# Attention and a gated MLP on one core: the early stage's operations held back and issued in one written order

## The chip, the cores and the metric

The kernel runs on one core of one Trainium2 chip. The time is the device time of one execution in microseconds (us). A core has five engines that run their own queues of instructions side by side and wait for one another by semaphores: TensorE (PE; its weight loads are listed apart as PEld), VectorE (DVE), ScalarE (ACT), GpSimd (POOL) and SyncE (SP), which issues most of the DMAs. A few DMAs are issued from ACT's queue.

## What is computed

Block-causal attention over 8 batches and 8 heads, 576 positions, head size 64, blocks of 64; its output, as 4608 tokens of width 512, goes through a gated MLP and an output projection.

```python
def _attn_ref(q, k, v):                      # (8, 8, 576, 64)
    scores = scale * np.matmul(q, k.transpose(0, 1, 3, 2))
    mask = block_i >= block_j                # blocks of 64 positions
    scores = np.where(mask, scores, -1000000000.0)
    scores = scores - np.max(scores, axis=-1, keepdims=True)
    attn = np.exp(scores)
    attn = attn / (np.sum(attn, axis=-1, keepdims=True) + 1e-09)
    return np.matmul(attn, v).astype(np.float32)

def _moe_ref(x, w1, w2, w3, w_out):          # x: (4608, 512)
    a = x @ w1
    b = x @ w2
    h = a * b @ w3
    return (h @ w_out).astype(np.float32)
```

The kernel folds the last two products: it computes `w3 @ w_out` once (1024 x 512), and the MLP then is `((x@w1)*(x@w2)) @ (w3@w_out)`.

## The kernel before

**Tiles and stages.** The work goes by pairs of heads, n = 0 to 31 (8 batches of 4 pairs); a pair has two halves, j = 0 and 1, one for each head. Pairs 0 to 3, the first batch, are the *early stage*: while they run, the weights arrive and are taken apart. From pair 4 on, the *late stage*, every step of attention is mixed with steps of the MLP of the batch before.

**Attention of a pair.** `shift_mask` casts k and q to bf16 (`kb`, `qd`, L166 on ACT), makes the block maxima of the scores in six groups of matmuls (`mx`, L192, in a ring of two `psq` banks), which DVE reduces into `m` (L196, L198). One transpose on PE (`mt`, L200) and a scaling on ACT (`ms`, L202) turn them into a row, and `shift` sends 2.2 KB of it by DMA into row slots of `qk0` and `qk1` (L218), so that the scores come out with the maximum taken off. These steps for pair n+1 stand within pair n. `prep_qk` makes the high and low parts of q and k (`qk0`, `qk1`: L166, DMAs L232 and L233, subtraction L235). The scores (`s`, L265, two banks `pss`) are two matmuls for each tile; the second reads the row that the DMA brought. ACT exponentiates them (in the early stage into `pe`, L273). In the early stage `pv_early` multiplies them with v in plain float32 (`x`, L304, one bank pair `psx`); `take_early` (L344 to L346) takes the sums and the result out, `norm` (L355 to L358) and `finish_x` (L367, L368) normalize and split it.

**Weights.** They come in 40 units of 512 KB (L143, issued on SP, ring `wraw` of 5), and each is put together by five steps of `load_w`: the scaled upper half (`wy`, ACT L150), a byte on ACT (L151) and one on POOL (L152) into one of two `wbits` tiles, and the join on DVE (L153). `w1` and `w2` are then split into two parts (POOL L161, DVE L162); `w_out` lies in `wo`, and `w3` in blocks `w`, two in the ring.

**The folded product.** `gen_prod` runs eight blocks m = 0 to 7 of eight matmuls each (L407, tiles `w0` to `w7`, two banks `psm`); `wh` and `wl` (L410 on ACT, L411 on DVE) take a block out.

**What sets the order.** PE's order is that of the program in the whole kernel (`manual_schedule` for PE alone): `EARLY_PLAN` says for each pair and half in which order the steps come, one letter a step; C is a step of the weights and W a quarter of a product block. The other four engines are ordered by the tile scheduler; the early stage's steps other than C and W run under `high_priority(offset=0)`. Buffers come from tile pools, which hand the next tile a buffer when its last user is done.

```python
            for step in EARLY_PLAN[n][j].split() if early else PLAN[j].split():
                if step in "CW":
                    fill(weights if step == "C" else prod, 1)
                    continue
                with tc.high_priority(offset=0) if early else nullcontext():
```

Of the kernel before, what the change touches and what calls it, by code (L numbers as in the profile page):

```python
# [8 lines left out]
F32 = mybir.dt.float32  # L9
# [7 lines left out]
AX = mybir.AxisListType  # L17
PSUM = bass.MemoryType.PSUM

P = 128  # L20
# [39 lines left out]
)  # L60

DELAY = 3

CAST = (0, 1, 1, 1)


@with_exitstack
def block_causal_attention__then__gated_mlp_kernel(ctx, tc, qkv, consts, ident_in, w1, w2, w3t, wout, out_t):
    nc = tc.nc
    w1, w2, w3t, wout = (w.bitcast(I32) for w in (w1, w2, w3t, wout))  # L70
# [30 lines left out]
    def load(n):  # L101
        t = raws.tile([P, RAW], F32, tag="raw", name=f"raw{n}")
        src = qkv[n // NPAIR, n % NPAIR]
        for cs in (slice(S, 2 * S), slice(0, S), slice(2 * S, RAW)) if n == 0 else (slice(0, RAW),):
            nc.sync.dma_start(out=t[:, cs], in_=src[:, cs])
        raw_of[n] = t

    load(0)
    for t, tag in enumerate(("tr", "x32")):
        cst = work.tile([P, S], F32, tag=tag, name=f"cst{t}")  # L110
# [27 lines left out]
    def load_w(dst, src):  # L138
        t = tl["early"].tile([P, 1024], I32, tag="wraw", name="wraw", bufs=5)
        y = tl["early"].tile([P, 512], F32, tag="wy", name="wy", bufs=4)  # L140
        bits = tl["bits"][tl["unit"] % 2]
# [32 lines left out]
    def shift_mask(n):  # L174
        r = raw_of[n]
        rqk = r[:, 0 : 2 * S].rearrange("p (t s) -> p t s", t=2)
        kb = work.tile([P, S], BF16, tag="kb", name=f"kb{n}")
# [4 lines left out]
        m = work.tile([P, 32], F32, tag="m", name=f"m{n}")  # L182

        groups = [((7, 0, 512),), ((8, 0, 512),), ((0, 0, 64), (6, 0, 448)), ((1, 0, 128), (5, 0, 384)),
                  ((2, 0, 192), (4, 0, 320)), ((8, 512, 576), (3, 0, 256))]
        for g, parts in enumerate(groups):
            t = ps_q.tile([P, 512], F32, tag="psq", name=f"mx{n}_{g}")
            at = 0
            done = []
            for i, a, b in parts:  # L190
                sc = t[:, at : at + b - a]
                nc.tensor.matmul(sc, qd[:, i, :], kb[:, a:b], start=True, stop=True)  # L192
                done.append((sc, 9 if a else i))
                at += b - a
            for sc, col in done:
                nc.vector.reduce_max(m[:, col : col + 1], sc, axis=AX.X)  # L196
            yield
        nc.vector.tensor_tensor(out=m[:, 8:9], in0=m[:, 8:9], in1=m[:, 9:10], op=ALU.max)  # L198
        mt = ps_q.tile([P, 512], F32, tag="psq", name=f"mt{n}")
        nc.tensor.transpose(out=mt[0:NB, 0:P], in_=m[:, 0:NB], identity=ident)  # L200
        ms = work.tile([64, P], F32R, tag="ms", name=f"ms{n}")[32 : 32 + NB]
        nc.scalar.mul(out=ms, in_=mt[0:NB, 0:P], mul=-1.0)  # L202
# [52 lines left out]
    def s_tile(n, j, parts, p_early):  # L255
        t = ps_s.tile([P, 512], F32, tag="pss", name=f"s{n}_{j}")
        at = 0
# [83 lines left out]
    def take_early(n, j, xps, x32, rr):  # L341
        o, x = own[j], oth[j]
        tr = work.tile([P, S], F32, tag="tr", name=f"tr{n}_{j}")
        nc.vector.transpose(tr[o], xps[x, 384:960])  # L344
        nc.vector.tensor_scalar_add(rr[o], tr[o].rearrange("p (b c) -> p b c", c=32)[:, :, 0], 1e-9)
        nc.scalar.copy(x32[o], xps[o, 384:960])  # L346
# [7 lines left out]
    def norm(n, x32, rr):  # L354
        nc.vector.reciprocal(rr, rr)  # L355
        rb = work.tile([P, S], F32, tag="tr", name=f"rb{n}")
        nc.vector.transpose(rb, rr.unsqueeze(2).broadcast_to([P, S // 32, 32]))
        (nc.gpsimd if n < 2 else nc.vector).tensor_tensor(out=x32, in0=x32, in1=rb, op=ALU.mult)  # L358

    def finish_x(n, x32):  # L360
        for h in range(2):
            at = (2 * n + h) % 12
            pool, bufs = (xpool, 8) if at < 8 else (tl["late"], 4)
            xh = pool.tile([P, HALF], F32R, tag="xh", name=f"xh{n}_{h}", bufs=bufs)
            xl = pool.tile([P, HALF], F32R, tag="xl", name=f"xl{n}_{h}", bufs=bufs)
            src = x32[:, h * HALF : (h + 1) * HALF]
# [7 lines left out]
    def gen_w(wp):  # L374
# [4 lines left out]
        def w3(m):  # L379
            assert done[0] >= m - 1  # L380
            t3_of[m] = wp.tile([P, NF, P], F32, tag="w3", name="w3", bufs=2)
            for h in range(2):
# [19 lines left out]
    def gen_prod():  # L402
        wo = tl["wo"]
        for m in range(NF):
            acc = ps_m.tile([P, 512], F32, tag="psm", name=f"w{m}")
            for k in range(NF):
# [61 lines left out]
    def pair(n):  # L468

        early = n < EARLY  # L470
        x32 = work.tile([P, S], F32, tag="x32", name=f"x32_{n}")
        rr = work.tile([P, S // 32], F32, tag="rr", name=f"rr{n}")
        part = None if early else work.tile([P, 2, S // 32], F32, tag="part", name=f"part{n}")
# [4 lines left out]
        for j in range(2):  # L478
            xps = ps_x.tile([P, 1024], F32, tag="psx", name=f"x{n}_{j}")
            p_early = wp.tile([P, 1600], F32, tag="pe", name=f"pe{n}_{j}") if early else None  # L480
            tiles = s_tiles(n, j, p_early)
            pvs = (pv_early if early else pv)(n, j, xps, p_early)
            delay = DELAY if n == NPAIR and j == 0 else 0
            for step in (EARLY_PLAN[n] if early else PLAN)[j].split():
                if step in "CW":
                    fill(weights if step == "C" else prod, 1)
                    continue
                with tc.high_priority(offset=0) if early else nullcontext():
                    if step == "S":
                        fill(tiles, 1)  # L490
                    elif step == "F":
                        if delay:
                            delay -= 1
                        else:
                            fill(mlp, 1)
                    elif step == "M":
                        fill(masks, 1)
                    elif step == "A":
                        fill(next_qk, 1)
                    elif step == "B":  # L500
                        fill(own_qk, 1)
                    elif step in "UV":
                        fill(pvs, 1)
                    elif step == "R":
                        sums(n, j, part)
                    elif step == "N" and early:
                        take_early(n, j, xps, x32, rr)
                    elif step == "N":
                        take(n, j, xps, x32)
                    elif step == "T":  # L510
                        if not early:
                            total(n, part, rr)
                        norm(n, x32, rr)
                        finish_x(n, x32)
                    elif step == "Q" and not last:
                        if n + 1 != NPAIR:
                            prep_v(n + 1, j)
                        if j == 1 and n + 2 < NN:
                            load(n + 2)
# [69 lines left out]
```

## Time and profile before

| | |
|---|---|
| time, median of 3 runs | 969.47 us (968.91 to 970.46) |
| the profiled execution's own time | 970.15 us |
| its span in the profile | 968.3 us |
| instructions | 18335 |
| DMA packets, bytes | 31303, 79.81 MB |

The profile is of one execution. Times in it are in us from the span's start. A row of the timeline gives start, duration, engine, line and operation, the output tile and its inputs (buffer numbers left out), partitions x elements, type and how many instructions the row stands for; in square brackets is how long the engine was idle ahead of it and what ended that. A float32 matmul on PE is listed as two records. "Granted clock" (PEclk) is the share of TensorE's full clock in that stretch.

### The profile page before, as it was taken

What the parts mean: (1) busy time and instruction counts of PE and PEld (TensorE: products, weight loads), DVE (VectorE), ACT (ScalarE), POOL (GpSimd) and SP (SyncE); (2) the same over time, 40 slices, a digit from 0 to 9 for tenths busy, and PEclk for the clock granted to TensorE, in tenths of its full rate; (3) what the DMA queues carried; (4) which work ended last, traced back from release to release, by engine and by line L of the source; (5) the groups of instructions that cost most, each with busy time, mean ns of one, the idle gap of its engine ahead of it and who ended that gap; (6) DMA issues with size and microseconds to landing.
All of it is one profiled execution on the core that took longest, in us unless ns stands there. A gap on an engine that the chain in (4) does not pass through costs nothing.

```text
span 968.3 us, 18335 instructions
## 1 busy us (share of the span) xinstructions
PE 938.8 (97%) x6624; PEld 878.7 (91%) x6624; DVE 692.3 (72%) x1230; ACT 556.6 (57%) x1451; POOL 617.5 (64%) x605
## 2 busy tenths in 40 slices
PE   3898899999999999999999999999999999999998
PEld 1454469999999999999999999999999999999998
DVE  6787767788777777787787777777887777774100
ACT  7768736556565556565656555565555656553221
POOL 6766737677766767677776767676777667672211
PEclk9899999999999999999999999999999999999999
DMA  8976512212212221321222222222122122100000
GB/s 303 305 230 204 158 51 64 86 32 72 76 58 82 65 88 52 88 65 47 66 76 64 71 81 64 78 61 88 33 69 75 58 82 64 50 13 26 7 20 26
DMA packets 31303, 79.81 MB, mean 82 GB/s; under 512 B 5356, under 2 KB 13676, under 8 KB 31212
## 3 DMA queue, kind: packets, MB, share of 16 engines
q1 hardware_dynamic: 29788, 76.26, 25.7%
q10 hardware_dynamic: 1424, 2.38, 1.0%
q8 instruction: 52, 0.85, 0.4%
q14 instruction: 39, 0.32, 0.1%
HBM read 50.76 MB, written 9.44 MB: 62 GB/s over the span
## 4 chain that ended last, share of the span: by engine, by line
PE 89%; ACT 3%; DVE 3%; POOL 2%; issue 1%; DMA 1%; ACTq 0%; SPq 0%; DVEq 0%; POOLq 0%
PE ab L426 42%; PE o L442 21%; PE s L265 9%; PE x L320 9%; PE mx L192 4%; PE w L407 2%; POOL wbits L152 1%; ACT wbits L151 1%; ACT wy L150 1%; PE x L304 1%; DVE m L196 1%; ACT pe L273 1%; DMA qk<-ms 1%; DVE w L153 0%; PE tot L337 0%
## 5 line engine op out<-in xcount | busy, mean ns | idle before, releaser
L286 POOL TENSOR_TENSOR rsum<-rsum,p 128x448 f32<-128x448 f32 x224 | 185.8, 829 | 86.8 <-ACT p L280 78.3
L283 DVE TENSOR_TENSOR pl<-p,ph 128x448 fp32r<-128x448 f32 x168 | 149.4, 903 | 59.9 <-ACT ph L281 59.0
L435 POOL TENSOR_TENSOR gl<-g,gh 128x288 fp32r<-128x288 f32 x128 | 114.4, 894 | 121.9 <-ACT gh L434 121.9
L265 PE MATMUL s<-qk 128*128 128x288 f32 (+4 forms) x768 | 155.2, 311 | 6.1 <-ACT pe L273 3.6
L235 POOL TENSOR_TENSOR qk<-raw,qk 64x1152 fp32r<-64x1152 f32 x58 | 155.0, 2673 | 8.6 <-issue 5.6
L426 PE MATMUL ab<-xh,w2h 128*128 128x288 f32 x512 | 153.8, 300 | 0.0
L442 PE MATMUL o<-gh,wh 128*128 128x288 f32 x512 | 153.6, 300 | 0.0
L426 PE MATMUL ab<-xh,w1h 128*128 128x288 f32 x512 | 151.1, 295 | 0.0
L426 PE MATMUL ab<-xl,w2h 128*128 128x288 f32 x512 | 151.0, 295 | 0.0
L426 PE MATMUL ab<-xl,w1h 128*128 128x288 f32 x512 | 151.0, 295 | 0.0
L426 PE MATMUL ab<-xh,w1l 128*128 128x288 f32 x512 | 150.9, 295 | 0.0
L426 PE MATMUL ab<-xh,w2l 128*128 128x288 f32 x512 | 150.9, 295 | 0.0
L442 PE MATMUL o<-gh,wl 128*128 128x288 f32 x512 | 150.9, 295 | 0.0
L442 PE MATMUL o<-gl,wh 128*128 128x288 f32 x512 | 150.8, 295 | 0.0
L434 ACT CAST gh<-g 128x288 fp32r<-128x288 f32 x128 | 55.4, 433 | 143.1 <-DVE g L433 143.0
L265 PEld LDWEIGHTS s<-qk 128*128 128x128 f32 (+1 forms) x768 | 116.0, 182 | 17.9 <-ACT pe L273 9.4
L281 ACT ACTIVATE ph<-s 128x288 fp32r<-128x288 f32 x336 | 131.5, 393 | 0.0
L196 DVE TENSOR_REDUCE m<-mx 128x1 f32<-128x64 f32 (+3 forms) x320 | 128.4, 447 | 2.2 <-PE mx L192 0.2
L280 ACT ACTIVATE p<-s 128x448 f32<-128x448 f32 x224 | 85.4, 381 | 51.2 <-PE s L265 50.4
L283 DVE TENSOR_TENSOR pl<-rsum,ph 128x288 fp32r<-128x288 f32 x112 | 75.6, 676 | 49.6 <-ACT ph L281 45.6
L320 PE MATMUL x<-ph,vs 128*128 128x128 f32 x336 | 110.4, 329 | 0.0
L433 DVE TENSOR_TENSOR g<-ab,a 128x288 f32<-128x288 f32 x128 | 56.6, 442 | 69.8 <-PE ab L426 69.0
(76 smaller groups left out, 2180.4 us busy)
## 6 DMA issues: line engine op xcount, KB each, us to landing
raw<-in_qkv SPq DMA_DIRECT2D x31, 896.0 KB
qk<-qk SPq DMA_DIRECT2D x108, 144.0 KB
out_t<-o SPq DMA_DIRECT2D x64, 144.0 KB
wraw<-in_w3t SPq DMA_DIRECT2D x16, 512.0 KB
wraw<-in_w SPq DMA_DIRECT2D x16, 512.0 KB
wraw<-in_wout SPq DMA_DIRECT2D x8, 512.0 KB
qk<-qk ACTq DMA_DIRECT2D x16, 144.0 KB
qk<-ms SPq DMA_DIRECT2D x54, 2.2 KB
```

What stands on the lines that cost most here:

```text
L196: nc.vector.reduce_max(m[:, col : col + 1], sc, axis=AX.X)
L235: (nc.gpsimd if "late" in tl or n * j else nc.vector).tensor_tensor(out=qk[j][o, 2:4], in0=rqk[o], in1=qk[j][o, 0:2], op=ALU.subtract)
L265: nc.tensor.matmul(t[ks, at : at + q1 - q0], qk[j][:, k, kr], qk[j][:, q, q0:q1], start=(s == 0), stop=(s == 1))
L280: nc.scalar.activation(p32, t[ks, at : at + w], AF.Exp, scale=SCALE)
L281: nc.scalar.activation(ph[ks, o : o + w], t[ks, at : at + w], AF.Exp, scale=SCALE)
L283: nc.vector.tensor_tensor(out=low, in0=p32, in1=ph[ks, o : o + w], op=ALU.subtract)
L286: nc.gpsimd.tensor_tensor(out=r, in0=r, in1=p32, op=ALU.add)
L320: nc.tensor.matmul(xps[:, to : to + w], v[:, c, :], pr[:, a : a + w], start=(u < 2 and s == 0), stop=(u in (0, len(PV) - 1) and s == len(p ...
L426: nc.tensor.matmul(t[:, 0:HALF], l[:, c, fs], r, start=(c == 0 and s == 0), stop=(c == NC - 1 and s == 2))
L433: nc.vector.tensor_tensor(out=g32, in0=acc[1][:, 0:HALF], in1=a32, op=ALU.mult)
L435: nc.gpsimd.tensor_tensor(out=gl[:, f, :], in0=g32, in1=gh[:, f, :], op=ALU.subtract)
L442: nc.tensor.matmul(t[:, 0:HALF], l[:, f, es], r[:, f, :], start=(f == 0 and s == 0), stop=(f == NF - 1 and s == 2))
```

## The change

In the early stage the name `nc` no longer stands for the core but for a recorder, `Held`. Each call on it is appended to a list and not issued; 761 calls are collected. Tiles are not made at that point either: `new` returns a `Later`, which is resolved when a held call that uses it is issued, and `slot` then gives it a buffer of a ring in turn: two for `raw`, `pss`, `psm`, `psq` and `w3`, five for `wraw`, four for `wy`, eight for `xh` and `xl`, one for all others. After the early stage's program has run through, all calls are issued in the order that `ORDER` lists, under `manual_schedule` for the other four engines, so that the order of each engine in this part is that of `ORDER`. The late stage follows with the real `nc`, as before. `high_priority` is gone. In the changed kernel every held call carries the line of `Held.__call__`, L123, and tiles of a ring have one name for all their uses (`psm` for `w0` to `w7`, `psq` for `mx` and `mt`, `psx` for `x`, `m` and `ms` without a number).

```diff
-from contextlib import ExitStack, nullcontext
+from contextlib import ExitStack
...
+OTHERS = {mybir.EngineType.Activation, mybir.EngineType.DVE, mybir.EngineType.Pool, mybir.EngineType.SP}
...
+ORDER = [int(k) for k in """
+0 10 1 2 11 3 6 12 9 44 58 46 48 13 71 63 53 41 40 72 68 14 93 43 5 15 42 20 21 16 70 7 47 76 79 22 45 23 4 59 17 18 49 19 32 33 8 50 34 28 29 35 30
...
+""".split()]
+
+RING = {"raw": 2, "pss": 2, "psm": 2, "psq": 2, "wraw": 5, "wy": 4, "w3": 2, "xh": 8, "xl": 8}
...
+class Later:
+
+    def __init__(self, make):
+        self.make, self.made = make, None
+
+    def get(self):
+        if self.made is None:
+            self.made = self.make()
+        return self.made
+
+    def __getitem__(self, key):
+        return Later(lambda: self.get()[key])
...
+class Held:
+
+    def __init__(self, target, calls):
+        self.target, self.calls = target, calls
+
+    def __getattr__(self, name):
+        return Held(getattr(self.target, name), self.calls)
+
+    def __call__(self, *a, **k):
+        self.calls.append(lambda: self.target(*map(got, a), **{n: got(v) for n, v in k.items()}))
...
-    nc = tc.nc
+    calls = []
+    nc = Held(tc.nc, calls)
+
+    rings = collections.defaultdict(list)
+
+    def new(pool, shape, dtype, tag, **k):
+        if not isinstance(nc, Held):
+            return pool.tile(shape, dtype, tag=tag, **k)
+        return Later(lambda: slot(pool, shape, dtype, tag, **k))
+
+    def slot(pool, shape, dtype, tag, name, **k):
+        ring = rings[tag]
+        n = RING.get(tag, 1)
+        t = ring[-n] if len(ring) >= n else pool.tile(shape, dtype, tag=tag, name=tag, **k)
+        ring.append(t)
+        return t
...
-                with tc.high_priority(offset=0) if early else nullcontext():
-                    if step == "S":
-                        fill(tiles, 1)
+                if step == "S":
+                    fill(tiles, 1)
...
     fill(weights, 100)
     fill(prod, 100)
+    with tc.manual_schedule(engines=OTHERS):
+        for k in ORDER:
+            calls[k]()
+    nc = tc.nc
+    raw_of.update((n, got(t)) for n, t in raw_of.items())
+    ms_of.update((n, got(t)) for n, t in ms_of.items())
+    x_of.update((k, tuple(map(got, t))) for k, t in x_of.items())
     wstack.close()
     open_late()
```

The order of the instructions at the places that matter most, first TensorE's at the end of pair 0, before (`s0_1`, `pe0_1`, `ve1` and `x0_1` are scores, exponentials, v and result of its half 1; `mt1` is the transpose of pair 1's maxima, `w0` the first block of the folded product):

```order
L265 MATMUL s0_1_322<-qk1_87 128x320 x2
L265 MATMUL s0_1_343<-qk1_87 128x192 x2
L265 MATMUL s0_1_343<-qk1_87 64x64 x2
L304 MATMUL x0_1_282<-pe0_1_283,ve1_157 128x128
L304 MATMUL x0_1_282<-pe0_1_283,ve1_157 128x448 x2
L200 MATMUL mt1_355<-ident_81,m1_211 9x128
L304 MATMUL x0_1_282<-pe0_1_283,ve1_157 128x320
L304 MATMUL x0_1_282<-pe0_1_283,ve1_157 128x192
L304 MATMUL x0_1_282<-pe0_1_283,ve1_157 128x64
L407 MATMUL w0_383<-wo_108,w3_298 128x512 x4
```

And now, where `w0` stands in the ring tile `psm_280` and `ve0` belongs to half 0 of pair 0:

```order
L123 MATMUL psx_210<-pe_202,ve0_97 128x320
L123 LDWEIGHTS qd_90
L123 MATMUL psq_138<-kb_119,qd_90 128x64
L123 LDWEIGHTS qd_90
L123 MATMUL psq_138<-kb_119,qd_90 128x256
L123 MATMUL psm_280<-wo_94,w3_274 128x512 x8
L123 MATMUL psq_141<-ident_81,m_150 9x128
L123 LDWEIGHTS qd_90
L123 MATMUL psq_138<-kb_119,qd_90 128x128
L123 MATMUL psm_312<-wo_94,w3_289 128x512
```

The whole first block stands now within PV of half 0, ahead of `mt1` and of all scores of half 1; the second block (`psm_312`) begins right behind it, one matmul at a time.

TensorE's order where the early stage ends and pair 4 begins (`mt4` is the transpose of pair 4's maxima, `s4_0` its first scores), before:

```order
L200 MATMUL mt4_1063<-ident_81,m4_914 9x128
L304 MATMUL x3_1_978<-pe3_1_979,ve1_157 128x320
L304 MATMUL x3_1_978<-pe3_1_979,ve1_157 128x192
L304 MATMUL x3_1_978<-pe3_1_979,ve1_157 128x64
L407 MATMUL w6_1031<-wo_108,w3_857 128x512 x4
L407 MATMUL w7_1095<-wo_108,w3_1034 128x512 x8
L265 MATMUL s4_0_1129<-qk0_86 128x288 x2
```

And now:

```order
L123 MATMUL psx_210<-pe_202,ve1_98 128x320
L123 MATMUL psx_210<-pe_202,ve1_98 128x192
L123 MATMUL psx_210<-pe_202,ve1_98 128x64
L123 MATMUL psm_312<-wo_94,w3_289 128x512 x8
L123 MATMUL psq_138<-ident_81,m_150 9x128
L340 MATMUL s4_0_929<-qk0_86 128x288 x2
```

The transpose has moved from ahead of PV's last three matmuls to behind the last block of the product, and stands directly ahead of pair 4's scores.

ScalarE's order at the same place (`ms4` is the scaled row, `vs0` and `vs1` are pair 4's v, `wh` the high part of a block of the folded product), before:

```order
L202 ACTIVATE ms4_1065<-mt4_1063 9x128
L218 DMA qk0_86<-ms4_1065 1x9x64
L346 COPY x32_3_872<-x3_1_978 64x576
L218 DMA qk1_87<-ms4_1065 1x9x64
L367 CAST xh3_0_1081<-x32_3_872 128x288
L410 CAST wh_84<-w6_1031 128x512
L367 CAST xh3_1_1085<-x32_3_872 128x288
L410 CAST wh_84<-w7_1095 128x512
L166 CAST vs0_1113<-raw4_831 128x5x64
```

And now:

```order
L123 COPY x32_109<-psx_210 64x576
L308 DMA qk1_87<-qk1_87 64x576
L123 CAST xh_891<-x32_109 128x288
L123 CAST xh_894<-x32_109 128x288
L123 CAST wh_84<-psm_312 128x512
L123 ACTIVATE ms_186<-psq_138 9x128
L241 CAST vs0_913<-raw_101 128x5x64
L123 DMA qk0_86<-ms_186 1x9x64
L241 CAST vs1_914<-raw_101 128x5x64
L293 DMA qk1_87<-ms_186 1x9x64
```

The scaling and its two DMAs stood ahead of `wh` of blocks 6 and 7; they stand now behind the last `wh`, and the casts of pair 4's v lie between them.

More of the change, by code (lines that the diff above doesn't have):

```diff
@@ L101, in load @@
     def load(n):
-        t = raws.tile([P, RAW], F32, tag="raw", name=f"raw{n}")
+        t = new(raws, [P, RAW], F32, tag="raw", name=f"raw{n}")
         src = qkv[n // NPAIR, n % NPAIR]
@@ L109, in block_causal_attention__then__gated_mlp_kernel @@
     for t, tag in enumerate(("tr", "x32")):
-        cst = work.tile([P, S], F32, tag=tag, name=f"cst{t}")
+        cst = new(work, [P, S], F32, tag=tag, name=f"cst{t}")
         nc.sync.dma_start(out=cst[0:D], in_=consts[:, t * S : (t + 1) * S])
@@ L138, in load_w @@
     def load_w(dst, src):
-        t = tl["early"].tile([P, 1024], I32, tag="wraw", name="wraw", bufs=5)
-        y = tl["early"].tile([P, 512], F32, tag="wy", name="wy", bufs=4)
+        t = new(tl["early"], [P, 1024], I32, tag="wraw", name="wraw", bufs=5)
+        y = new(tl["early"], [P, 512], F32, tag="wy", name="wy", bufs=4)
         bits = tl["bits"][tl["unit"] % 2]
@@ L176, in shift_mask @@
         rqk = r[:, 0 : 2 * S].rearrange("p (t s) -> p t s", t=2)
-        kb = work.tile([P, S], BF16, tag="kb", name=f"kb{n}")
+        kb = new(work, [P, S], BF16, tag="kb", name=f"kb{n}")
         cast(n, kb, rqk[:, 1, :], CAST[1])
@@ L181, in shift_mask @@
         yield
-        m = work.tile([P, 32], F32, tag="m", name=f"m{n}")
+        m = new(work, [P, 32], F32, tag="m", name=f"m{n}")
         groups = [((7, 0, 512),), ((8, 0, 512),), ((0, 0, 64), (6, 0, 448)), ((1, 0, 128), (5, 0, 384)),
@@ L186, in shift_mask @@
         for g, parts in enumerate(groups):
-            t = ps_q.tile([P, 512], F32, tag="psq", name=f"mx{n}_{g}")
+            t = new(ps_q, [P, 512], F32, tag="psq", name=f"mx{n}_{g}")
             at = 0
@@ L255, in s_tile @@
     def s_tile(n, j, parts, p_early):
-        t = ps_s.tile([P, 512], F32, tag="pss", name=f"s{n}_{j}")
+        t = new(ps_s, [P, 512], F32, tag="pss", name=f"s{n}_{j}")
         at = 0
@@ L342, in take_early @@
         o, x = own[j], oth[j]
-        tr = work.tile([P, S], F32, tag="tr", name=f"tr{n}_{j}")
+        tr = new(work, [P, S], F32, tag="tr", name=f"tr{n}_{j}")
         nc.vector.transpose(tr[o], xps[x, 384:960])
@@ L355, in norm @@
         nc.vector.reciprocal(rr, rr)
-        rb = work.tile([P, S], F32, tag="tr", name=f"rb{n}")
+        rb = new(work, [P, S], F32, tag="tr", name=f"rb{n}")
         nc.vector.transpose(rb, rr.unsqueeze(2).broadcast_to([P, S // 32, 32]))
@@ L404, in gen_prod @@
         for m in range(NF):
-            acc = ps_m.tile([P, 512], F32, tag="psm", name=f"w{m}")
+            acc = new(ps_m, [P, 512], F32, tag="psm", name=f"w{m}")
             for k in range(NF):
@@ L487, in pair @@
                     continue
-                with tc.high_priority(offset=0) if early else nullcontext():
-                    if step == "S":
-                        fill(tiles, 1)
[L491 to L519, printed above, removed]
@@ new lines, in pair @@
+                if step == "S":
+                    fill(tiles, 1)
+                elif step == "F":
+                    if delay:
+                        delay -= 1
+                    else:
+                        fill(mlp, 1)
+                elif step == "M":
+                    fill(masks, 1)
+                elif step == "A":
+                    fill(next_qk, 1)
+                elif step == "B":
+                    fill(own_qk, 1)
+                elif step in "UV":
+                    fill(pvs, 1)
+                elif step == "R":
+                    sums(n, j, part)
+                elif step == "N" and early:
+                    take_early(n, j, xps, x32, rr)
+                elif step == "N":
+                    take(n, j, xps, x32)
+                elif step == "T":
+                    if not early:
+                        total(n, part, rr)
+                    norm(n, x32, rr)
+                    finish_x(n, x32)
+                elif step == "Q" and not last:
+                    if n + 1 != NPAIR:
+                        prep_v(n + 1, j)
+                    if j == 1 and n + 2 < NN:
+                        load(n + 2)
```

22 lines of the change are left out of this document (13 added, 9 removed), and 19 rows, old and new, of the table ORDER.

## The prediction

> **What bounds the kernel now.** I read the page's busy shares and its chain first, then where TensorE (PE) waits.
>
> ```profile
> span 968.3 us, 18335 instructions
> PE 938.8 (97%) x6624; PEld 878.7 (91%) x6624; DVE 692.3 (72%) x1230; ACT 556.6 (57%) x1451; POOL 617.5 (64%) x605
> PE   3898899999999999999999999999999999999998
> PEclk9899999999999999999999999999999999999999
> PE 89%; ACT 3%; DVE 3%; POOL 2%; issue 1%; DMA 1%; ACTq 0%; SPq 0%; DVEq 0%; POOLq 0%
> ```
>
> PE is busy 97% of the span and makes up 89% of the chain that ended last. Each digit of the second row is one slice of 24.2 us, and the only slices below 9 are 0, 1, 3, 4 and the last one. In the view of PE's waits no wait of PE stands between 150 us and the end. So the time can change only before the late stage begins, or at its seam, and the late stage's own order is the same in both kernels. **The question is when its first scores (pair 4) start, and whether they run on.** In the profile of before that start is 136.24 us, the last row here (start, duration, engine, line, tile):
>
> ```profile
> 5.93 1.01 PE L192 MATMUL mx<-kb,qd 128*128 128x512 bf16 x2 [5.93 <-ACT qd L166]
> 20.80 0.61 PE L192 MATMUL mx<-kb,qd 128*128 128x512 bf16 x1 [4.24 <-ACT qd L166]
> 37.07 3.70 PE L407 MATMUL w<-wo,w 128*128 128x512 f32 x8
> 126.24 10.57 PE L407 MATMUL w<-wo,w 128*128 128x512 f32 x24
> 136.24 0.96 PE L265 MATMUL s<-qk 128*128 128x288 f32 x3
> ```
>
> What comes before is poor in work until the weights are there, and rich after. In the stretches below the columns are length, busy time and count of PE, weight load, DVE, ACT, POOL, then granted clock, DMA share, GB/s:
>
> ```profile
> 0.00:20.00 20.00, 4.91 (x15) 2.05 (x15) 13.07 (x21) 13.36 (x22) 13.36 (x20) 1.00 0.84 308
> 31.00:37.00 6.00, 5.23 (x17) 3.15 (x17) 4.90 (x7) 3.46 (x9) 4.37 (x4) 0.72 1.02 326
> 46.00:51.00 5.00, 5.00 (x17) 3.21 (x17) 2.57 (x5) 4.36 (x8) 1.86 (x2) 0.69 0.65 200
> 66.76:136.24 69.48, 63.90 (x215) 33.30 (x215) 52.24 (x81) 42.97 (x87) 40.40 (x38) 1.00 0.52 154
> ```
>
> In the first 20 us PE works 4.91 us, and the DMA is 0.84 full with the weights. From 66.76 us on PE is the limit; what it has before is wasted. Its waits between the first product at 37.07 and the late stage are these (total, times, longest), 8.5 us together:
>
> ```profile
> PE mx L192 <- DVE m L196: 3.0, 3, 2.0
> PE mx L192 <- ACT qd L166: 2.1, 1, 2.1
> PE s L265 <- ACT pe L273: 1.9, 3, 1.2
> PE s L265 <- DMA qk<-ms: 1.5, 2, 1.0
> ```
>
> **The change, part by part.** The set of early instructions is the same; what changes is their place, on all five engines. I therefore count when the first product can start, what PE has left from there, and what the end costs.
>
> *First product.* w0 needs both halves of w3's first block. They were written on VectorE (DVE) by 28.48 (27.81+0.67) and 30.93 (30.26+0.67):
>
> ```profile
> 27.81 0.67 DVE L153 SCALAR_TENSOR_TENSOR w<-wy,wbits 128x512 int32<-128x512 int32 x1
> 28.51 0.79 DVE L344 STREAM_TRANSPOSE tr<-x 64x576 f32<-64x576 f32 x1
> 29.60 0.40 DVE L345 TENSOR_SCALAR rr<-tr 64x18 f32<-64x18 f32 x1
> 30.26 0.67 DVE L153 SCALAR_TENSOR_TENSOR w<-wy,wbits 128x512 int32<-128x512 int32 x1
> 31.32 1.60 DVE L235 TENSOR_TENSOR qk<-raw,qk 64x1152 fp32r<-64x1152 f32 x1
> ```
>
> Before, w0 waits in PE's order behind the scores and the attention-times-values product (PV) of half 1. In the new order it stands behind mask 1 and ahead of its transpose mt1. On DVE the 1.60 of pair 1's subtraction now stands ahead of the second w3 half, and the transpose and sum of pair 0 (0.79, 0.40) behind it: 30.93+1.60−1.19 = 31.3. The first half has one 0.67 weight step less ahead. PE runs the eight matmuls in order of k, so the first four can start on the first half. I take 30.7 for the start, between 28.5 (first half as before, no more ahead of it) and 33.7 (31.3 with another 1.60 and 0.79 of DVE ahead of it). This fills PE time in the stretch 31 to 37, where the clock was 0.72.
>
> *What is left on PE behind it.* From 37.07 to 136.24 are 99.17 us, of which 8.5 are waits, and the cold clock costs about 1.7: 5 x (1−0.69) = 1.55 at 46 to 51, and 0.15 around it. That leaves 89.0 of work at full clock. What stood ahead of w0 and now stands behind it comes on top: scores of half 1 of pair 0, its PV, the last two PV matmuls of half 0, and mt1. From rows of the same kinds in a later pair:
>
> ```profile
> 88.28 0.67 PE L265 MATMUL s<-qk 128*128 128x448 f32 x2
> 88.86 0.54 PE L265 MATMUL s<-qk 128*128 128x320 f32 x2
> 89.24 1.88 PE L407 MATMUL w<-wo,w 128*128 128x512 f32 x4
> 93.53 1.89 PE L304 MATMUL x<-pe,ve 128*128 128x128 f32 x6
> 95.26 0.27 PE L200 MATMUL mt<-ident,m 128*9 128x128 f32 x1
> 96.69 5.42 PE L407 MATMUL w<-wo,w 128*128 128x512 f32 x12
> ```
>
> The 448-wide tile takes 0.58 (88.28 to 88.86) and the next 0.38 (to 89.24); with the part of the 288-wide and short tiles that stood ahead, estimated at 1.3 from these, about 2.2. PV is 93.53 to 96.69 less the transpose, 3.1 with what starts it. The two short PV matmuls are some 0.4, the transpose 0.1 as it lies between others: 5.8 in sum, so 94.8 us of work.
>
> *Waits inside it.* The new order keeps every dependence, with the same rings, so I bound them by 0 and the 8.5 of before. Going down the five queues of the new order by the durations of such rows, I find 4.1: x's bank, which pair 1's PV gets after the transpose and copy of pair 0 (1.5); mask 3, whose casts stand behind weight steps on ScalarE (ACT) (1.2); pair 3's scores (0.7); w7 (0.5); 0.2 scattered. The cold clock at the first product is between 0 and 6 x (1−0.72) = 1.7, and I take 0.85, the middle, as no row is nearer to one end.
>
> The last product would then end at 30.7+94.8+4.1+0.85 = 130.45, **5.8 us ahead** of the 136.24 of before.
>
> *The seam gives it back.* This term is the one that decides. Before, the transpose mt4 of pair 4's row maxima stands at 124.81, and the rest of PV with 24 product records (10.57 in the row above) is PE's cover while ACT scales it and two small DMAs carry it into qk0 and qk1. Afterwards mt4 stands behind all of w7, directly ahead of s4, and nothing is left for PE: s4's second matmul needs that DMA, and every later instruction of PE is behind it.
>
> ```profile
> 124.81 0.27 PE L200 MATMUL mt<-ident,m 128*9 128x128 f32 x1
> 126.67 0.27 ACT L202 ACTIVATE ms<-mt 9x128 fp32r<-9x128 f32 x1 [3.92 <-PE x L304]
> 126.97 0.80 ACTq L218 DMA_DIRECT2D qk<-ms  x1
> ...
> 136.84 0.59 ACT L410 CAST wh<-w 128x512 fp32r<-128x512 f32 x1 [5.25 <-PE w L407]
> 137.32 0.82 ACT L166 CAST vs<-raw 128x320 fp32r<-128x320 f32 x2
> ```
>
> ```profile
> 37.34 1.31 ACTq L218 DMA_DIRECT2D qk<-ms  x1
> 41.35 0.64 PE L265 MATMUL s<-qk 128*128 128x288 f32 x3 [0.45 <-DMA qk<-ms]
> 45.78 0.61 PE L192 MATMUL mx<-kb,qd 128*128 128x512 bf16 x1 [2.07 <-ACT qd L166]
> ```
>
> ACT's queue there is wh of w7, ms4, a cast of vs0, the DMA. From w7's end: 0.60 until wh starts (136.84−136.24), wh 0.59, ms 0.27, the issue 0.80, and a flight of 2.70 (41.35 less 37.34+1.31, the one row where PE waited for such a DMA to land): 4.96. The vs0 cast lies beside the issue, as a copy did at 127.8. Mt4 and s4's first matmul run meanwhile, about 0.3, so PE waits 4.65; bounds 2.5 (ms ahead in time, flight 1) and 6 (the vs0 cast in full, a slower flight). By a wait of 2.07 at 45.78 the clock fell to 0.69 for the 5 us that follow, so this one can cost 0 to 1.55 more; I take 0.8, the middle. Seam: 5.45.
>
> The Trainium skill says ("DMA: Bandwidth & Descriptors", Anatomy of one DMA) that a DMA has a fixed cost of about 2.0 us. The trace's flight of 2.70 came between stretches with a DMA share of 1.02 and 0.65; with 2.0 for it the sum would be 0.7 lower, 968.4.
>
> *Sum.* −5.8 + 5.45 = −0.35. The profiled run took 970.15 (1.85 around its span), so 969.8 for it; it lay 0.68 above the median 969.47, so **969.1** beside the median. That is no change: within 0.2% is within 1.94 us, about what a measurement of this kernel can tell from none.
>
> **Rivals.** (1) *As forecast*, 47%: gain of 3 to 8 against a seam of 4 to 6, so −4 to +3, 965.5 to 972.5; of this 13 faster, 22 same, 12 slower. (2) *The order holds better*, 25%: the waits inside it are 1 instead of 4.1, with no cold clock, so the gain is 5.8+3.1+0.85 = 9.75, and the flight is short on idle DMA queues (share 0.01 at the end, as in the row below), so the seam costs 3: 969.47−6.75 = 962.7. For it speaks that the DMA share falls from 0.65 to 0.01; against it that weight steps fill ACT and DVE at 62 to 75% between 66.76 and 136.24 in the row above.
>
> ```profile
> 116.00:126.00 10.00, 10.00 (x40) 5.67 (x40) 9.33 (x18) 6.07 (x13) 3.60 (x5) 1.00 0.01 2
> ```
>
> (3) *Slower*, 20%: one mechanism, the mask casts of the next pair on ACT. The 2.07 wait of PE at 45.78 was for such a cast (qd), and it drew a cold clock of 1.55. In the new order these casts stand behind whole weight units, at fixed places; ACT cannot take them earlier. If twice the casts come after PE has ended the product beside them, that is 2 x 3.6 = 7.2 instead of the 4.1+0.85 forecast, and with the seam at its upper end plus cold clock, 7.5: −5.8+2.25+7.5 = +3.95 and, with the first product at 31.3, 4.5: about 974. It decides from where ACT reaches the next pair's k cast later than PE reaches the end of the third block's second pair of matmuls. (4) *The change does not bite*, 3%: the products start as before, the new places only swap idle time; 969.5. (5) *The first product runs cold in full*, 5%: PE had 4.91 us of work in its first 20, and at 31 to 37 the clock was 0.72, so the filler that is set into that stretch can run at it for 6 us: 1.7 and not 0.85, 970.0.
>
> The Trainium skill says ("TensorE: Matmul & The Clock Gate", Part 1: The HAM clock gate) that PE runs at half rate until about 3.4 us of sustained work and falls back when idle. The trace agrees that idle is followed by less than full clock (0.72 and 0.69), so by it rival 5 and the upper end of the seam would hold.
>
> **How the numbers follow.** The bounds: start of the first product 28.5 to 33.7 (−2.2, +3.0), waits 0 to 8.5 (−4.1, +4.4), cold clock −0.85 to +0.85, seam 2.5 to 7.5 (−2.95, +2.05). Their ends do not fall together; most of rivals 2 and 3 lies within 962 to 976, and 2 in 10 stays outside. Chances: faster 13 + 25 = 38%; same 22 + 3 + 5 = 30%; slower 12 + 20 = 32%.
>
> **What would show it.** In the profile of the changed kernel: the first `w<-wo` matmul at 30.7 (past 34 and the filler failed); PE's waits between it and w7 at about 4; w7's end near 130.5; a wait of about 4.65 of s4's scores for the DMA of ms and a clock below 1.00 after it; then the late stage without a wait, as long as before. The prediction is wrong if s4 runs on without a wait (the seam then costs nothing, and the gain stays), or if the casts of kb and qd hold PE by over 3 us twice.

## The result: 1% slower, and the profile after

The changed kernel took 981.64 us (median of 4 runs, 981.04 to 982.51), the kernel before 969.97 beside it: a ratio of 1.0103, 95% interval 1.0076 to 1.0129. The range of the prediction ended at 976. From the page of the profile of the changed kernel:

```profile
span 980.5 us, 18332 instructions
PE 946.4 (97%) x6624; PEld 882.9 (90%) x6624; DVE 696.4 (71%) x1230; ACT 559.7 (57%) x1451; POOL 621.0 (63%) x605
PE   4888979999999999999999999999999999999998
PEclk9898999999999999999999999999999999999999
```

PE's busy time is up by 7.6 us for the same 6624 matmuls, and the clock row has a second slice below 9: some of the work ran at a lower granted clock. PE's waits up to the late stage, by the view of waits (total, times, longest):

```profile
PE psm L123 <- DVE w L123: 9.0, 4, 4.2
PE psq L123 <- ACT qd L123: 6.5, 1, 6.5
PE psq L123 <- DVE m L123: 4.8, 5, 1.7
PE pss L123 <- DVE qk L123: 3.6, 1, 3.6
PE s L340 <- DMA qk<-ms: 2.6, 1, 2.6
```

The costliest wait is a new one: products (`psm`) wait for joined weights (`w`), where before no product ever waited for them. The timeline of PE shows where:

```profile
31.33 4.88 PE L123 MATMUL psm<-wo,w 128*128 128x512 f32 x7 [1.95 <-DVE w L123]
68.93 7.13 PE L123 MATMUL psm<-wo,w 128*128 128x512 f32 x16 [1.31 <-DVE w L123]
80.49 3.78 PE L123 MATMUL psm<-wo,w 128*128 128x512 f32 x4 [4.17 <-DVE w L123]
135.89 8.83 PE L123 MATMUL psm<-wo,w 128*128 128x512 f32 x16 [1.58 <-DVE w L123]
147.54 1.09 PE L340 MATMUL s<-qk 128*128 128x288 f32 x3 [2.58 <-DMA qk<-ms]
```

Two rows have 16 records of the same kind, and take 7.13 and 8.83: the second ran partly at half clock. The stretches in which the granted clock was half, and around them the whole of what the prediction summed, from the first product to the end of the last (columns as before: length, PE, weight load, DVE, ACT, POOL, clock, DMA share, GB/s):

```profile
31.33:34.60 3.27, 3.27 (x4) 1.51 (x5) 2.87 (x6) 2.80 (x5) 3.09 (x3) 0.50 1.02 359
31.33:144.56 113.23, 102.56 (x334) 55.10 (x335) 82.85 (x126) 73.37 (x147) 67.25 (x60) 0.93 0.55 172
61.91:65.32 3.41, 3.38 (x9) 2.30 (x10) 0.98 (x2) 1.86 (x6) 0.00 (x0) 0.50 0.00 0
78.97:85.80 6.83, 5.31 (x8) 2.18 (x9) 1.87 (x4) 3.51 (x7) 4.21 (x5) 0.50 0.69 244
137.00:140.42 3.42, 3.42 (x6) 1.35 (x5) 3.36 (x5) 0.64 (x1) 1.31 (x1) 0.50 0.02 4
```

The first wait of 1.95 lies ahead of the first product, the others behind it. 113.23 less 102.56 busy is 10.67 of waits. Half of the busy time at half clock is lost, (3.27+3.38+5.31+3.42)/2 = 7.69, so the work is 94.87 at full clock. With these the account closes:

| term | forecast | measured |
|---|---|---|
| start of the first product | 30.7 | 31.33 |
| work behind it, at full clock | 94.8 | 94.87 |
| waits within it | 4.1 | 10.67 |
| half clock | 0.85 | 7.69 |
| end of the last product, against 136.24 | −5.8 | +8.3 |
| seam | 5.45 | 3.86 |
| change of the span | −0.35 | +12.2 |

The seam is from the timeline: from the start of the first late scores to that of the second score tile the kernel before takes 136.24 to 138.81, and the changed one 144.59 to 151.02. The second tile, before and after:

```profile
138.81 1.16 PE L265 MATMUL s<-qk 128*128 128x448 f32 x4
151.02 0.85 PE L340 MATMUL s<-qk 128*128 128x448 f32 x4
```

2.58 of the 3.86 is the wait, the rest the half clock behind it. From there to the end both take 829.5 us, so the late stage itself cost nothing.

Why are the joins late? ScalarE's timeline around the third block's first weight unit (unit 14, counted from 0):

```profile
46.55 0.66 ACT L123 ACTIVATE wy<-wraw 128x512 f32<-128x512 f32 x1
64.86 0.43 ACT L123 ACTIVATE pe<-pss 128x192 f32<-128x192 f32 x2 [1.55 <-PE pss L123]
65.19 0.77 ACT L123 ACTIVATE wbits<-wraw 128x512 fp8e4<-128x512 uint8 x1
...
68.91 0.79 ACT L123 ACTIVATE wbits<-wraw 128x512 fp8e4<-128x512 uint8 x1 [1.25 <-DVE w L123]
```

The unit's first step ran at 46.55, its byte step on ScalarE at 65.19, behind all exponentials of pair 1. For these 18.6 us it held a load buffer and one of the two byte tiles; the steps of units 16 (the row at 68.91), 18 and 20 came behind it. Whether this one unit held them up, or the place of each, is the question of an experiment below. The join of unit 14 was slow as well, beside a subtraction on GpSimd:

```profile
65.71 2.62 POOL L123 TENSOR_TENSOR qk<-raw,qk 64x1152 fp32r<-64x1152 f32 x1 [4.07 <-DVE qk L123]
65.99 2.88 DVE L123 SCALAR_TENSOR_TENSOR w<-wy,wbits 128x512 int32<-128x512 int32 x1 [0.43 <-ACT wbits L123]
```

Most such joins took 0.69. At that length this one would have ended at 66.68, ahead of the end of PE's work at 67.62, so by this estimate the wait of 1.31 needed both, the late byte step and the slow join. SyncE's queue:

```profile
43.61 4.34 SPq L123 DMA_DIRECT2D wraw<-in_w  x2
53.26 0.33 SPq L123 DMA_DIRECT2D raw<-in_qkv  x1
65.99 0.83 SPq L123 DMA_DIRECT2D wraw<-in_w3t  x2
```

From 47.95 to 65.99 no weight load was issued. PE was busy 21.18 of the 23 us from 45 to 68, 4.28 of them with the product, none of it behind 54.44, and the rest with attention, of pair 0's second half and then of pair 1. No further weights were fetched meanwhile, and the waits for them came afterwards.

### The profile page after: what moved, and what is told of

The parts are those of the page before. It is cut to its first block, busy times and chain, and to the rows that moved or that the text cites. A ratio compares the mean times of both kernels' runs of the same rounds, so it can differ in the third digit from the quotient of the medians.

```text
span 980.5 us, 18332 instructions
## 1 busy us (share of the span) xinstructions
PE 946.4 (97%) x6624; PEld 882.9 (90%) x6624; DVE 696.4 (71%) x1230; ACT 559.7 (57%) x1451; POOL 621.0 (63%) x605
## 4 chain that ended last, share of the span: by engine, by line
PE 91%; DVE 3%; POOL 2%; issue 1%; DMA 1%; ACT 1%; SPq 0%; POOLq 0%; DVEq 0%; ACTq 0%
PE ab L501 42%; PE o L517 21%; PE s L340 9%; PE x L395 9%; PE psm L123 4%; PE mx L267 4%; POOL wbits L123 1%; PE psx L123 1%; DVE w L123 1%; DMA wraw<-in_wout 1%; PE pss L123 1%; DVE qk L123 0%; PE psq L123 0%; SPq L123 0%; POOL w2h L123 0%
## 5 line engine op out<-in xcount | busy, mean ns | idle before, releaser
L310 POOL TENSOR_TENSOR qk<-raw,qk 64x1152 fp32r<-64x1152 f32 x55 | 147.2, 2676 | 2.8 <-DVE qk L241 0.8
L340 PE MATMUL s<-qk 128*128 128x288 f32 (+4 forms) x672 | 129.8, 301 | 2.6 <-DMA qk<-ms 2.6
L271 DVE TENSOR_REDUCE m<-mx 128x1 f32<-128x512 f32 (+1 forms) x270 | 107.7, 448 | 1.7
L340 PEld LDWEIGHTS s<-qk 128*128 128x128 f32 (+1 forms) x672 | 100.2, 180 | 3.9 <-DMA qk<-ms 2.8
```

Source lines behind the costliest of these rows:

```text
L310: (nc.gpsimd if "late" in tl or n * j else nc.vector).tensor_tensor(out=qk[j][o, 2:4], in0=rqk[o], in1=qk[j][o, 0:2], op=ALU.subtract)
L340: nc.tensor.matmul(t[ks, at : at + q1 - q0], qk[j][:, k, kr], qk[j][:, q, q0:q1], start=(s == 0), stop=(s == 1))
```

## Experiments

Four theories stood against one another. **A**: weight steps at late, fixed places starve the products, PE then waits, its clock falls, and the seam comes on top. **B**: TensorE's new order itself costs, whoever orders the others. **C**: the fixed buffers, or a lack of time on ScalarE. **D**: the half clock has another cause than waits. Ratios are to the kernel before, measured beside each; its median there was 969.97 to 971.61, so two experiments are better compared by their ratios than by their times. Edits of `ORDER` name the calls by what they do.

**The seam alone**, in the changed kernel.

```diff
-... w7[k2] w7[k3] ... w7[k7] ... wh(7) ms4-transpose ms4-scale ms4-DMA
+... w7[k2] w7[k3] ms4-transpose (x32 copy) ms4-scale ms4-DMA w7[k4] ... w7[k7] ... wh(7)
```

> One edit in the changed kernel's order: the transpose of pair 4's maxima goes into the middle of the last product block, its scaling and DMA behind the copy of pair 3's result on ScalarE. Theory A (the seam costs 2.58 us of wait and about 1.3 of cold clock, on top of what is lost earlier): the wait of the first late scores for the DMA goes, the clock stays at 1.00 behind it, the time falls by 3.9, to 977.7. Rival B (the seam's wait only swaps with the wait for the last weight unit, which lands at 139.9 anyway): the time falls by less than 1.

978.83 us, ratio 1.0071 (1.0044 to 1.0098). In the profile the wait for the DMA is gone. From the first late scores to the second score tile it takes 143.60 to 146.17, 2.57 as in the kernel before, so the whole 3.86 is saved. The ratio fell by 0.3%, with intervals that overlap. An experiment in the kernel before, further down, shows the same price from the other side.

**Weight units 14 to 23 earlier**, with an error.

```diff
 wy(14) ... wy(16)
+byte-step(14) ... join(14) byte-steps(16) join(16) split(16) byte-steps(18) join(18) split(18) wy..split(19)
+load(20) load(21) load(22) load(23)
 ... last exponentials of pair 1
-byte-step(14) join(14) load(20) load(21) byte-steps(16) ... steps(20, 21)
+steps(20, 21)
```

> The changed kernel with 21 weight steps and four weight DMAs of units 14 to 23 moved ahead in the order, TensorE's own order untouched. Theory A (in the changed order the ScalarE byte step of unit 14 stands at 65.2, 18.6 us behind its first step; it holds a load buffer and one of the two byte tiles, so units 16, 18, 20 and 21 are late and TensorE waits 1.31 for the third block and 4.17 for the fourth, with 2.7 of cold clock behind): both waits go, w3 starts by 77, and the time falls by 5 to 8, to 974 to 977. Rival B (TensorE's order itself, pair 1 without products, is what costs): the joins come earlier but TensorE only waits elsewhere, within 2 us of 981.6. Rival C (ScalarE is short of time there, so weight steps set ahead delay the exponentials by as much): waits for pe take the place of those for w, again within 2 us.

984.37 us, ratio 1.0130. Here the loads of units 20 and 21 overwrite those of 14 and 17 ahead of their last steps, so units 14 and 17 are put together from the wrong bytes, and the steps waited for loads that should have come behind them. It says nothing on the theories.

**The same, each load behind the last reader of its buffer.**

> As the edit of units 14 to 23 before, with the four loads each behind the last step that reads the buffer that it takes (in the run before two stood ahead of it, so ScalarE and GpSimd waited for loads that they should have preceded, and pe came 5.6 us late). Theory A (late weight steps hold up the third and the fourth block): the joins of units 14 and 16 come by 52 and 58, those of 20 and 21 by 71, the waits of 1.3 and 4.2 for w and the half clock at 79 to 86 go: 974 to 977. Rival B (whatever is set earlier, TensorE's written order leaves it without other work somewhere): waits of the same size at other tiles, 980 or more.

977.55 us, ratio 1.0063 (1.0044 to 1.0082), 0.4% or 4 us better than the change and 0.55 above the range of theory A. PE's waits from the first product to the late stage, the five largest:

```profile
PE s L340 <- DMA qk<-ms: 2.6, 1, 2.6
PE pss L123 <- ACT pe L123: 2.5, 2, 2.1
PE pss L123 <- DMA qk<-ms: 2.4, 1, 2.4
PE psm L123 <- DVE w L123: 1.6, 1, 1.6
PE psx L123 <- ACT pe L123: 1.4, 2, 0.9
```

The waits of 1.31 and 4.17 for `w` are gone, with the half clock at 79; in their place stand one of 2.1 for `pe` and one of 2.4 for pair 2's DMA of `ms`, which the moved steps now precede. A holds for the cause of these two waits. They and the half clock behind them were 1.31+4.17+2.66 = 8.1, of which 4 came back; the new waits, which B foretold, took the rest. Rival C's lack of time on ScalarE is not what the change shows: it was busy 14.31 of the 23 us from 45 to 68.

**Unit 14 alone**: its byte step, its join and load 20.

> The changed kernel with three of the moved steps alone: the late byte step and the join of unit 14, and the load of unit 20 that waits for unit 14's buffer. If the one held unit is the cause (the narrow form of theory A): units 16, 18, 20 and 21 follow by themselves, the wait of 4.17 for the fourth block shrinks below 1.5, 976 to 978 as with all the moved steps. If each later step is held by its own place in the four queues (the wide form): only the wait of 1.31 for the third block goes, the wait of about 4 stays, 979.5 to 982.

980.15 us, ratio 1.0098 (1.0082 to 1.0114): no gain that can be told from the change, as the wide form has it. The wait of 1.31 went, one of 4.0 for the fourth block stayed. So unit 14 alone is not the cause of the larger wait: the later units have places of their own behind pair 1's work.

**The four engines left to the scheduler, PE's new order kept.**

```diff
-    with tc.manual_schedule(engines=OTHERS):
-        for k in ORDER:
-            calls[k]()
+    for k in ORDER:
+        calls[k]()
```

> The changed kernel with TensorE's written order, but the other four engines left to the tile scheduler (the calls are issued in the written order, without the manual schedule for the four). Theory A (the fixed places of weight steps on the four engines cost): the scheduler takes weight steps when they are ready, waits for w fall below 4 us in sum, 972 to 977. Rival B (TensorE's order costs): 980 or more, whoever orders the four.

985.70 us, ratio 1.0148 (1.0110 to 1.0187). A was half right and its time was wrong: the one wait for `w` that is left, 1.6, is that at the first product, but others came (from there to the late stage):

```profile
PE psx L123 <- ACT x L123: 5.4, 2, 3.2
PE pss L123 <- ACT pe L123: 4.5, 4, 1.8
PE psx L123 <- ACT pe L123: 1.9, 2, 1.2
PE psm L123 <- DVE w L123: 1.6, 1, 1.6
```

Waits for `w` inside the product are gone, and the kernel is no faster. I read this so: PE's new order runs pair 1 densely, with no product to fill the time between its steps. When weight steps go first on ScalarE and VectorE, pair 1 waits for `pe` and `x`; when pair 1's steps go first, as in the change, the products wait for `w`. That the fixed places are only one way to pay for PE's order is argued and not shown, for this run also lacks the priorities of before, and the scheduler without them may simply have ordered badly.

**The fixed buffers alone**: held calls in the program's own order, PE as before, the rest scheduled with the priorities of before.

```diff
-        for k in ORDER:
-            calls[k]()
+    for first, call in calls:
+        with tc.high_priority(offset=0) if first else nullcontext():
+            call()
```

> The held calls issued in the program's own order, with the steps that had priority before given it again, the four engines left to the scheduler as before: what is left of the change is the fixed buffers in turn. TensorE's order is that of before. Theory A: the buffers cost nothing, 968.5 to 971. Rival C (fixed buffers make the engines wait for one another where the pool would have handed out another buffer): 974 or more.

972.49 us, ratio 1.0016 (1.0001 to 1.0030), between the two expectations: at most 0.3%, so C's buffers are not the cause. The run before has the scheduler and the buffers too. PE's order, the missing priorities and the order of issue, which differ, are together worth 985.70 − 972.49 = 13.2 us.

**The tail**: seam edit, and units 38 and 39 joined ahead of the last splits and reductions.

> The seam edit, and with it units 38 and 39 (the last block of w3) joined ahead of the splits of units 36 and 37 and of the last mask reductions. Theory A: the wait of 1.58 ahead of the last block and the half clock behind it go too, 3.3 together, on top of the 3.9 of the seam: 974 to 975.5. Rival B: the last exponentials and joins only change places, no gain over the seam edit alone, 977 to 979.

976.44 us, ratio 1.0058 (1.0038 to 1.0079), 1 us above the upper end of the expectation, and its interval overlaps that of the seam alone. The wait ahead of the last block fell from 1.58 to 0.86, and the half clock at 137 is gone; a wait of 0.69 for `wl` came behind it.

**All three edits.**

> Units 14 to 23 early, the tail and the seam, all three edits in one order. Theory A: 981.6 less 3.9, 3.3 and 5 to 8: 966 to 970, level with or just below the kernel before. Rival B: 975 or more.

973.02 us, ratio 1.0018 (1.0000 to 1.0036), between the two expectations. By the ratios the edits take back 0.85 of the 1.03%, about 8.2 us, and the rest can hardly be told from none. The profile is of its slowest execution, 977.36 us. It has waits of 2.9 for pair 2's `ms` and 2.1 for `pe` ahead of the late stage, and 2.2 for such DMAs within it, where the profile of the change has none.

**All three, and those two waits aimed at.** Units 16 and 18 behind pair 2's casts; pair 2's scaling and DMA ahead of the weight steps.

> The three edits of the run before in one order, with units 16 and 18 joined behind the casts and subtractions of pair 2 on VectorE and the scaling and DMA of pair 2's row maxima set ahead of the weight steps. In the run before TensorE still waited 2.07 for pe (with 6.8 us of half clock behind it, 3.3 of work lost) and 2.93 for the DMA of ms. Theory A (the place of each step in the four fixed queues decides, and each such wait can be moved out of the way): both go, the late stage starts 6 to 8 us earlier than in that run (at 133 to 135 where the kernel before has 136.24), 965 to 968. Rival B (with these waits gone the joins of the fifth to the eighth block are late in turn): 969 to 973.

974.32 us, ratio 1.0032 (1.0017 to 1.0047): not better, and above both expectations. Both waits went, but the late stage starts at 139.51 and not at 133 to 135. PE waits elsewhere instead, and mostly not for the joins that B named:

```profile
63.31 1.24 PE L123 MATMUL psx<-pe,ve 128*128 128x128 f32 x4 [1.59 <-ACT x L123]
76.63 1.98 PE L123 MATMUL psm<-wo,w 128*128 128x512 f32 x4 [1.99 <-DVE wl L123]
80.85 0.38 PE L123 MATMUL psq<-kb,qd 128*128 128x512 bf16 x1 [2.24 <-ACT qd L123]
```

No version that I tried beats the kernel before.

**PE kept warm**: 16 and 7 matmuls of 256 columns ahead of the fourth and the last block, overwritten by the block's first matmul.

```diff
+    for m, times in ((3, 16), (7, 7)):
+        for _ in range(times):
+            nc.tensor.matmul(acc_of[m][:, 0:256], ident, both, start=True, stop=True)
```

> The changed kernel with 16 matmuls of 256 columns, whose result is overwritten, set ahead of the fourth product block and 7 ahead of the last one, where TensorE waits 4.17 and 1.58 for w. If the half clock follows from TensorE's idle time (theory A): the half clock at 79 to 86 and at 137 to 140.4 goes, the waits become matmuls, and the time falls by about 4 (2.66 and 1.71 of work done at half speed), to 977 to 978.5. If the half clock comes for another reason (rival D): it stays, and the time rises by up to 3 where the added matmuls outlast the waits.

979.02 us, ratio 1.0069 (1.0035 to 1.0103), 0.3% below the change, with overlapping intervals; the execution profiled was its slowest, with a span of 980.5 like the change's. So a gain in time is not shown. What it shows for sure is the clock, in the same two stretches, first of the change, then of this run:

```profile
76.00:86.00 10.00, 5.83 (x11) 2.46 (x10) 4.38 (x8) 6.48 (x12) 7.04 (x7) 0.66 0.69 225
134.00:141.00 7.00, 5.42 (x10) 2.37 (x11) 6.87 (x9) 2.30 (x4) 3.54 (x2) 0.76 0.18 41
```

```profile
76.00:86.00 10.00, 10.00 (x40) 7.12 (x39) 4.20 (x7) 5.80 (x11) 6.20 (x7) 1.00 0.69 225
134.00:141.00 7.00, 7.00 (x23) 4.18 (x22) 6.81 (x11) 1.32 (x3) 3.05 (x1) 1.00 0.18 42
```

0.66 and 0.76 became 1.00: D falls, the half clock there follows from PE's idle time. The added matmuls outlast the waits (the fourth block starts at 82.25 instead of 80.49, the last at 136.39 instead of 135.89), so part of what the clock gains is lost again.

**The seam in the kernel before**: only the transpose of pair 4, its scaling and DMAs moved behind the last block.

```diff
-     "M S S A C W S M S A W C S W V V A M V V V Q N T W W"),
+     "M S S A C W S M S A W C S W V V A V V V Q N T W W"),
...
     fill(prod, 100)
+    with tc.high_priority(offset=0):
+        fill(held[0], 100)
```

> The kernel before, with one step alone moved: the transpose of pair 4's maxima, its scaling and its two small DMAs behind the last block of the product, as the change has them. Theory A (this place costs by itself): TensorE waits 2 to 3 us for the DMA of ms before the second late matmul, with up to 1.6 of cold clock: 972 to 974 beside 969.5. Rival B (the transpose costs only in the changed kernel, where the last weights are late): within 1 of the kernel before.

974.31 us, ratio 1.0038 (1.0024 to 1.0052). The row at the seam:

```profile
139.66 0.66 PE L265 MATMUL s<-qk 128*128 128x288 f32 x3 [2.94 <-DMA qk<-ms]
```

The first MLP matmul starts at 140.17 instead of 137.17, 3.0 later, which is this wait; the clock stayed full in this execution. It was the fastest of twelve, 972.81; the median is 3.7 above that of the kernel before, 0.3 above theory A's range. The seam costs by itself.

**The early product in the kernel before**: four matmuls of the first block ahead of the last scores of pair 0, half 1.

```diff
-    ("... ", "M S S A C S M S A C S V V A M V V V Q N T W W"),
+    ("... ", "M S S A C S M W W S A C S V V A M V V V Q N T"),
```

> The kernel before, with the first four matmuls of the first product block alone moved ahead of the last scores of pair 0, half 1, as the change does with the whole block. Theory A (the same work is done either way; an early product is worth only the wait that it covers, 1.4 us for pe at 31.8): 968 to 970. The prediction's reading (the earlier start of the product is worth several us by itself): 966 or less.

975.01 us, ratio 1.0041 (1.0028 to 1.0055): slower, and outside both expectations.

```profile
30.15 3.60 PE L407 MATMUL w<-wo,w 128*128 128x512 f32 x8
...
40.44 0.68 PE L304 MATMUL x<-pe,ve 64*128 64x64 f32 x2 [2.65 <-ACT pe L273]
41.05 0.61 PE L265 MATMUL s<-qk 128*128 128x288 f32 x1
45.05 1.06 PE L265 MATMUL s<-qk 128*128 128x288 f32 x3 [3.39 <-DMA qk<-ms]
```

The product started 6.9 us earlier than the 37.07 of before, and filled the wait that it was to fill. But then PE waited 6.4 us between 37 and 45, with nothing left to do while `pe` and the DMA were late (0.45 of wait for that DMA in the kernel before, 3.39 here), and from 39.13 to 49.37 the clock was half.

## Why the prediction was wrong, by its steps

*What bounds the kernel*: right. Only the time before the late stage and its seam changed, 12.2 us, and the late stage took as long as before.

*First product at 30.7*: right within 0.6, but in part by luck. The subtraction stood ahead of both halves of w3's block and not of the second alone, and the first half's join took 1.19 instead of 0.67 and ended at 31.28, where I had let it come early. The work of 94.8 behind it was right (94.87).

*Waits inside it, "I find 4.1"*: this is the step that failed, 10.67 measured. I walked the queues for x's bank, the mask casts, pair 3's scores and the last block, and gave the weights 0.5 in all. The waits for `w` are 1.31+4.17+1.58 = 7.06 of the 10.67. In the changed order the byte steps and joins of units 14, 16, 18, 20 and 21 stand behind pair 1's exponentials, which gives the first two (the first together with the slow join), and the joins of units 38 and 39 behind the last splits and reductions, which gives the third. The other 3.61 come near my 4.1 by chance: the mask casts cost nothing and x's bank 0.47, and the rest were waits for `pe` (0.98, 0.50 and 0.86) and `wl` (0.81). To see the weights I had to follow one unit through its five steps and its buffer, not each engine by itself. Taking the 8.5 of before as the upper end was wrong as well, for that bound came from an order in which no product waits for weights.

*Cold clock 0.85*: 7.69. I counted it once, at the first product, and not behind each wait of the new order, though the row at 45.78 had shown the price, 1.55 behind a wait of 2.07. Between them these two terms miss by 13.4 us.

*The gain of 5.8*: it was made of fewer waits (8.5 to 4.1) and a warmer clock (1.7 to 0.85), 5.25 together; the early product itself was worth 0.57 in my own sum, since what it overtakes comes behind it. In the order of the kernel before, four matmuls moved early were worth less than nothing; the whole block with the rest of the new order was not tried by itself. I should have asked what PE would have left to do at 37 to 80, once its filler was used up.

*Seam 5.45*: right as a mechanism, shown by the edit in either kernel; 3.86 measured. The wait was 2.58 and not 4.65, the half clock behind it 1.28 and not 0.8. The term that was too large is above all the flight of the small DMA, whose issue on ScalarE's queue was

```profile
145.66 0.79 ACTq L123 DMA_DIRECT2D qk<-ms  x1
```

It ended at 146.45 and PE went on at 147.54, 1.09 instead of 2.70. The 2.70 came from 38.65 to 41.35 in the kernel before, with a DMA share of 0.83; here the share was 0.01. From the start of the issue it is 147.54−145.66 = 1.88. The Trainium skill ("DMA: Bandwidth & Descriptors", Anatomy of one DMA) gives the fixed cost of about 2.0 us for a DMA issued from GpSimd's queue. I quoted it without that condition; the DMA here is issued from ScalarE's queue, so the 1.88 is near the figure, but no test of it.

*Rivals*: the one for slower was too mild, 974, and named the casts of the next pair; the casts (`qd`) cost nothing in the changed kernel once the first product runs. Rival 2 took the DMA share of 0.01 at the end of the kernel before as a sign of ease, and its short flight came true (1.09). But in the changed kernel the share fell to 0.00 already at 61.91 to 65.32, where weights were still to come.

What stays open: what the densely run pair 1 costs by itself. The 13.2 us hold PE's order as a whole and, with it, the missing priorities. The old order of PE with fixed queues on the other four engines wasn't tried.

## What to carry to other kernels

An order that keeps the busiest engine at 100% in one stage is no gain if it does so by using up the filler and holding back the stream that feeds the next stage: look for the last arrival of each input (here the last join, 122.6 before and 139.2 after), not at idle time. When queues are fixed by hand, follow one unit of data through all its steps and count how long it holds its buffers. And price each wait of TensorE with the half clock that can follow it.

## What the runs showed of the hardware

The half clock comes in whole stretches of 3.41 us, and it follows a stretch of that length in which PE was busy only in part; it need not be idle all through. Of the changed kernel:

```profile
58.50:61.91 3.41, 2.00 (x10) 1.27 (x8) 3.32 (x4) 1.73 (x5) 3.02 (x3) 1.00 0.37 87
65.32:68.73 3.41, 2.30 (x10) 1.35 (x8) 2.98 (x2) 1.10 (x2) 2.62 (x1) 1.00 0.58 157
75.56:78.97 3.41, 0.76 (x4) 0.30 (x2) 2.47 (x4) 3.41 (x7) 3.19 (x4) 1.00 0.64 171
133.59:137.00 3.41, 1.83 (x8) 0.99 (x7) 3.35 (x6) 1.76 (x3) 2.65 (x2) 1.00 0.19 43
```

After 2.00, 0.76 and 1.83 of 3.41 the next stretch was at half clock; after 2.30 it was not. In the run that aimed at two more waits, a stretch of 1.83 (61.44 to 64.86) was followed by full clock, and in the run with unit 14 alone one of 2.30 (55.98 to 59.39) by half clock, so a stretch that is about half busy can go either way. In all 14 profiles, from the first recorded clock (at 21 to 27 us) to 155 us, each of the 20 stretches at full clock with PE busy up to 41% was followed by half clock, 22 of the 52 with 42 to 67% were, and none of the 386 above that. The Trainium skill ("TensorE: Matmul & The Clock Gate", Part 1: The HAM clock gate) has the fall after an idle window of about 3.4 us; the length agrees, and the trace shows the fall also after windows that were more than half busy.

An instruction of VectorE was long when it ran beside a subtraction on GpSimd:

```profile
136.02 2.31 DVE L123 TENSOR_SCALAR rr<-tr 64x18 f32<-64x18 f32 x1
...
141.22 0.17 DVE L123 TENSOR_SCALAR rr<-tr 64x18 f32<-64x18 f32 x1
```

```profile
135.26 3.04 POOL L310 TENSOR_TENSOR qk<-raw,qk 64x1152 fp32r<-64x1152 f32 x1 [0.76 <-DVE qk L241]
```

The same tiny operation took 2.31 us where it ran beside the subtraction, and ended 0.03 us behind it (138.33 and 138.30); it took 0.17 alone. In the kernel before, one took 1.06 and ended 0.04 behind a subtraction (128.22 and 128.18). In the run with the seam alone moved in that kernel, the subtraction had ended at 126.42 when this operation began at 126.83, and it took 0.18. The join of unit 14 ended 0.54 behind a subtraction (68.87 and 68.33), and the corresponding join in the run with that unit moved 0.55 (50.82 and 50.27). So the time goes with the overlap; no run moved the subtraction alone.
